# First block solve on two 16-wide squares per block, with small TensorE products, and a new order of events

## The chip, the cores and the metric

The kernel runs on one core of one Trainium2 chip. The metric is the device time of the program in microseconds, the median of three runs.

## What is computed

Two stages, one after the other. The first is a delta-rule attention over 4 × 8 heads, 768 steps and head size 48; the second is a feed-forward block on its output, 3072 tokens × 384, with 2048 hidden columns.

```python
def _attn_ref(q, k, v, beta):
    k_n = k / (np.linalg.norm(k, axis=-1, keepdims=True) + 1e-06)
    state = np.zeros((B, H, D, D), dtype=np.float32)
    for t in range(S):
        kt, vt, bt = (k_n[:, :, t], v[:, :, t], beta[:, :, t, None])
        y[:, :, t] = np.einsum('bhd,bhde->bhe', q[:, :, t], state)
        v_old = np.einsum('bhde,bhd->bhe', state, kt)
        state = state + bt[:, :, :, None] * np.einsum('bhd,bhe->bhde', kt, vt - v_old)

def _moe_ref(x, w_in, w_out):
    h = x @ w_in
    sp = np.maximum(h, 0.0) + np.log1p(np.exp(-np.abs(h)))
    g = h * erf(sp)
    return (g @ w_out).astype(np.float32)
```

## The kernel before

The sequence is cut into 12 chunks c of 64 steps, and each chunk's recurrence is replaced by a triangular solve of 64 × 64 per head, followed by products. A tile holds the two halves of the heads on partitions 0 to 63 and 64 to 127 and 16 pairs of batch and head (BP) along the free axis. Two chunks share one solve (sg = 0 to 5).

**Solve and merge.** The 64 × 64 triangle is cut into two diagonal blocks of 32 × 32. For the first solve three transposes (`block_t`, L491) put the blocks into the tile gb, one block per partition as 32 × 32 elements; `solve_init` makes identities in xb. `solve_row(sg, s)` for s = 0 to 30 is one step of the substitution: a product into tmp (L507) and a sum into xb (L509), over (31 − s)(s + 1) elements per partition. Each of the 62 operations needs the one before it. The first solve goes to VectorE (DVE) unless the table ENG says GpSimd (POOL); the later ones to POOL unless ENG says DVE. `back_t` (L520) and `back_x` then bring the first solve's inverses back to the tile xm, on the partitions of the heads; later solves go through DRAM (`put_blocks`, `from_blocks2`). The off-diagonal 32 × 32 block follows by the merge: a transpose to T (`merge_t`, L550), 32 small products per chunk (`merge_e`, L561) into PSUM as pe, copies back to T, 32 products (`merge_z`, L576) as pz, copies to xm, and products with the keys (`merge_m`, L593) as pm, copied to xm with a minus (L600).

**State chain.** Per chunk, `chain_u` (L630) multiplies the state by the merged keys, DVE scales (L636), `chain_s` (L644) and a sum on DVE (L649) update the state z, and `chain_y` (L656, L660) makes the output y. z starts as a product of v and a scale (z<-v,nm).

**Feed-forward.** Twelve groups of 256 tokens, each after its chunk. Group 0 uses fp32 products (`ffn1` L866, `ffn2` L925). For the others, weights and activations are split into a high and a low f16 part, and each product is three f16 products (L871; L930 to L932). A unit of `ffn1` is 18 of them. The tokens' parts are xh and xl (L855), the nonlinearity runs on ACT (L893, L898), DVE (L903, L905) and POOL into H. Before that the raw weights are prepared in tasks between other work: signs (L738), bits (L743), maxima (L754), low parts (L819).

**What sets the order.** Every step is registered with `on(fn, ...)` and gets a number. The tuple ORDER lists the numbers in the order in which they are issued; each engine works through its own instructions in that order, and the tile framework adds the waits. ENG gives an engine to some of the numbers. Among the events are WF = 300 calls of `fill` (L265), a product of a zeroed tile whose result is not used. ORDER, ENG and WF come out of a planner outside this file.

## Time and profile before

| | us |
|---|---|
| runs | 619.26, 616.46, 619.92 |
| median | 619.26 |
| profiled execution, its own time | 618.54 |
| its span | 616.6 |
| TensorE busy in the span | 584.7 |
| of it the 300 fills | 59.4 |
| DVE, ACT, POOL busy | 458.6, 441.8, 271.1 |

The span runs from the first to the last instruction of the trace; 1.94 us of the execution lie around it. TensorE's busy time counts the fills, too. The mean granted TensorE clock is 0.98 of full speed.

### The profile page before, as it was taken

Reading aid. Unit: us, or ns where it says so; the run is one execution under the profiler, and the core shown is the slowest. Engines: PE = TensorE matmul, PEld = TensorE weight load, DVE = VectorE, ACT = ScalarE, POOL = GpSimd, SP = SyncE. Lnnn points to the kernel's source line nnn. Section 1 sums busy time; section 2 is a strip of 40 time slices with the busy share of each in tenths; the row PEclk is TensorE's granted clock in tenths of the full one; section 3 lists DMA queues with packets and bytes.
Section 4 is the critical chain, followed back from the end, with each engine's and each line's share of the span. In section 5 each row is a group of like instructions: output and inputs, shape, how many; then the busy total and the mean of one; then the engine's idle time right before and its main releaser. Section 6 shows DMA issues by size and latency. Waiting matters only on the chain.

```text
span 616.6 us, 24419 instructions
## 1 busy us (share of the span) xinstructions
PE 584.7 (95%) x10680; PEld 427.7 (69%) x10680; DVE 458.6 (74%) x1022; ACT 441.8 (72%) x628; POOL 271.1 (44%) x463
## 2 busy tenths in 40 slices
PE   7898889999999999999979999999999999999994
PEld 5554567777767776777757777777677777777662
DVE  5999978999988789776777986777885765665140
ACT  2447578798797688469656977769589878879460
POOL 7146234854758644876066753067532200001030
PEclk8889989999999999999998999999999999999998
DMA  9996499078244576284650616533054130101001
GB/s 282 275 307 148 139 243 244 28 158 189 56 117 106 121 169 151 72 191 108 137 107 8 158 38 131 107 65 90 2 121 96 33 94 2 28 3 27 2 13 39
DMA packets 79499, 67.84 MB, mean 110 GB/s; under 512 B 57696, under 2 KB 67040, under 8 KB 79136
## 3 DMA queue, kind: packets, MB, share of 16 engines
q1 hardware_dynamic: 79392, 66.28, 44.1%
q8 instruction: 84, 1.38, 1.0%
q14 instruction: 23, 0.19, 0.1%
HBM read 47.38 MB, written 17.83 MB: 106 GB/s over the span
## 4 chain that ended last, share of the span: by engine, by line
PE 69%; DVE 17%; ACT 4%; DMA 3%; issue 3%; POOL 2%; SPq 0%; DVEq 0%; ACTq 0%; POOLq 0%
PE ph L871 25%; PE pr L930 9%; PE pr L932 8%; PE pr L931 8%; PE pc L630 3%; PE pr L925 2%; DVE tmp L507 2%; PE pc L656 2%; DVE xb L509 2%; PE pc L644 2%; PE ph L866 2%; PE pm L593 2%; PE pc L660 1%; PE pg L409 1%; PE pe L561 1%
## 5 line engine op out<-in xcount | busy, mean ns | idle before, releaser
L871 PE MATMUL ph<-xh,w_in 128*128 128x256 f16 x1056 | 191.4, 275 | 2.3 <-DVE L L905 2.3
L871 PEld LDWEIGHTS <-w_in 128*128 128x128 f16 x1584 | 152.5, 99 | 30.1 <-issue 4.0
L255 ACT ACT_TABLE_LOAD x133 | 170.6, 1283 | 3.0 <-PEq L1150 0.7
L871 PE MATMUL ph<-xl,w_in 128*128 128x256 f16 x528 | 145.1, 275 | 0.9 <-DVE xl L855 0.9
L930 PE MATMUL pr<-w_out,H 128*128 128x384 f16 x352 | 115.1, 327 | 0.0
L931 PE MATMUL pr<-w_out,H 128*128 128x384 f16 x352 | 114.8, 326 | 0.0
L932 PE MATMUL pr<-w_out,H 128*128 128x384 f16 x352 | 114.8, 326 | 0.0
L212 POOL TENSOR_TENSOR H<-L,H 128x512 f16<-128x512 f32 x39 | 46.2, 1192 | 132.6 <-ACT H L217 64.5
L507 POOL TENSOR_TENSOR tmp<-gb,xb 128x255 f32<-128x255 f32 (+14 forms) x113 | 62.3, 551 | 80.4 <-DVE xb L509 69.1
L905 DVE SCALAR_TENSOR_TENSOR L<-ph,L 128x512 f32<-128x512 f32 x88 | 59.4, 685 | 51.4 <-ACT L L898 51.0
L893 ACT ACTIVATE L<-ph,xct 128x512 f32<-128x512 f32 x88 | 59.3, 687 | 52.9 <-PE ph L871 51.3
L509 POOL TENSOR_TENSOR xb<-xb,tmp 128x255 f32<-128x255 f32 (+14 forms) x113 | 64.7, 572 | 8.9
L265 PE MATMUL pr<-zero 128*128 128x384 f16 x300 | 59.4, 352 | 1.2 <-DVE zero L261 1.2
L898 ACT ACTIVATE L<-L 128x512 f32<-128x512 f32 x96 | 59.0, 626 | 0.8
L212 POOL TENSOR_TENSOR z<-v,nm 64x192 f32<-64x192 f32 x66 | 35.5, 537 | 54.1 <-DMA v<-vtok 30.8
L932 PEld LDWEIGHTS <-H 128*128 128x128 f16 x352 | 34.4, 98 | 22.8
L930 PEld LDWEIGHTS <-H 128*128 128x128 f16 x352 | 34.4, 98 | 20.2
L931 PEld LDWEIGHTS <-H 128*128 128x128 f16 x352 | 34.5, 98 | 18.2
L265 PEld LDWEIGHTS <-zero 128*128 128x128 f16 x300 | 29.4, 104 | 22.5 <-issue 5.8
L636 DVE TENSOR_TENSOR z<-pc,ga 64x192 f32<-64x192 f32 x94 | 33.4, 355 | 15.0 <-PE pc L630 12.7
L649 DVE TENSOR_TENSOR z<-pc,z 48x192 f32<-48x192 f32 x86 | 30.5, 354 | 12.1 <-PE pc L644 8.3
L212 DVE TENSOR_TENSOR H<-L,H 128x512 f16<-128x512 f32 x49 | 37.2, 770 | 1.5 <-ACT H L217 1.3
(191 smaller groups left out, 954.2 us busy)
## 6 DMA issues: line engine op xcount, KB each, us to landing
raw_out<-w_out SPq DMA_DIRECT2D x12, 512.0 KB, 5.6
d<-pp SPq DMA_DIRECT2D x10, 512.0 KB, 4.3
d<-A SPq DMA_DIRECT2D x20, 256.0 KB, 3.2
qp<-d SPq DMA_DIRECT2D x20, 256.0 KB, 5.2
k<-ktok SPq DMA_DIRECT2D x12, 384.0 KB, 4.7
kpg<-kT SPq DMA_DIRECT2D x24, 192.0 KB, 4.3
v<-vtok SPq DMA_DIRECT2D x48, 96.0 KB, 3.5
qp<-qT SPq DMA_DIRECT2D x24, 192.0 KB, 4.1
```

The source lines that it names most:

```text
L212: {"V": ve, "G": ge}[pick(d)].tensor_tensor(*a, **kw)
L255: se.add_instruction(mybir.InstLoadActFuncSet(name=nc.get_next_instruction_name(), act_func_set_id=i, ins=[], outs=[]))
L265: te.matmul(pr[1][:, :DM], zero[:, :P], zero[:, :DM], start=new, stop=new)
L507: eng.tensor_tensor(tv, g.unsqueeze(1).broadcast_to([P, ncol, nr]), Xv[:, :, s:s + 1].broadcast_to([P, ncol, nr]), op=ALU.mult)
L509: eng.tensor_tensor(Xv[:, :, s + 1:], Xv[:, :, s + 1:], tv, op=ALU.add)
L871: te.matmul(ph, w[:, i, kt * P:kt * P + P], G[x][:, :, ksl], start=(m == 0), stop=(m == 8))
L893: se.activation(unit(g, u), G["ph", u], AF.Softplus, bias=0.0, scale=G["ct"][:, part(EU * u):part(EU * u) + 1] if g >= GF else 1.0)
L898: se.activation(Lu, Lu, AF.Erf, bias=0.0, scale=1.0)
L905: ve.scalar_tensor_tensor(Lu, fg[g]["ph", u], HSC, Lu, op0=ALU.mult, op1=ALU.mult)
L930: te.matmul(G["po"][a], gh[:, o, asl], wout_h[:, i, :], start=(i == 0), stop=False)
L931: te.matmul(G["po"][a], gh[:, o, asl], wout_l[:, i, :], start=False, stop=False)
L932: te.matmul(G["po"][a], gl[:, o, asl], wout_h[:, i, :], start=False, stop=(i == NFF - 1))
```

## The change

The first solve no longer works on whole 32 × 32 blocks. Each block on a partition is cut into two diagonal squares of 16 × 16. `corner` is a view of the tile that takes both squares as one operand; for it the tiles gb and xb become 2 × 528 elements wide, so that the second square lies at the same distance (`wide`). `row16(s)`, s = 0 to 14, makes one step of both squares with two DVE operations over 2(15 − s)(s + 1) elements. The lower left square of each block is then computed on TensorE: `small_t` transposes the first half of xb to a tile T16; `small_e` makes 64 products per chunk with the gram block A01; `small_e2` copies the result to T16; `small_z` makes 64 products with the second square's inverse in xm; `small_z2` copies the results to xm, four copies per chunk. The merge of the 32-blocks follows as before. The later solves, sg = 1 to 5, keep `solve_row` on whole blocks.

All numbers of events shift, and ORDER and ENG are new throughout. The number of fills is 233. The lines of the new file are two lower than before up to the solve and 50 higher behind it.

```diff
-ORDER = (0, 1, 24, 27, 28, 16, 19, 22, 14, 11, 7, 5, 2, 10, 12, 15, 25, 20, 2233, 2234, 2235, 2236, 2237, 2238, 2239, 2240, 2241, 2242, 2243, 2244, 2245,
...
+ORDER = (0, 1, 2, 3, 4, 46, 15, 9, 12, 8, 19, 22, 24, 27, 28, 23, 29, 30, 31, 16, 32, 33, 34, 25, 20, 2232, 2233, 2234, 2235, 2236, 2237, 2238, 2239, 2240,
...
-ENG = {64: 'G', 65: 'G', 67: 'G', 68: 'G', 69: 'G', 77: 'G', 81: 'A', 82: 'V', 89: 'V', 92: 'A', 94: 'A', 101: 'V', 107: 'V', 110: 'V', 114: 'V', 118: 'A',
...
+ENG = {48: 'G', 49: 'G', 50: 'G', 51: 'G', 53: 'G', 55: 'G', 56: 'G', 58: 'G', 61: 'G', 68: 'A', 70: 'V', 78: 'V', 79: 'A', 86: 'A', 90: 'V', 92: 'V', 99:
...
-WF = 300
+WF = 233
...
@@ -469,7 +467,15 @@
         for hb in range(2):
             sp.dma_start(qp[c % 2][hb][r(1 - hb)], st[c]["d3"][r(hb)])
 
-    gb_t, xb_t = {}, {}
+    gb_t, xb_t, flat = {}, {}, {}
+
+    def wide(nm, sg):
+        flat[nm, sg] = at.tile([P, 2 * 528], F32, tag=nm, name=f"{nm}{sg}")
+        return flat[nm, sg][:, :1024].rearrange("p (a b) -> p a b", b=32)
+
+    def corner(nm):
+        v = flat[nm, 0].rearrange("p (b r) -> p b r", b=2)[:, :, :512]
+        return v.rearrange("p b (s t) -> p b s t", t=32)[:, :, :16, :16]
 
     def to_dram(c, h):
         if "d1" not in st[c]:
@@ -479,24 +485,36 @@
     def to_blocks(c, f):
         sg, i = divmod(c, 2)
         if sg not in gb_t:
-            gb_t[sg] = at.tile([P, 32, 32], F32, tag="gb", name=f"gb{sg}")
+            gb_t[sg] = wide("gb", sg)
         dv = st[c]["d1"].rearrange("(f s) h a t -> f (h a) s t", f=2)
         q0 = i * 64 + f * 32
         sp.dma_start(gb_t[sg][q0:q0 + 32], dv[f, :, :, f * 32:f * 32 + 32])
 
     def block_t(k):
         if 0 not in gb_t:
-            gb_t[0] = at.tile([P, 32, 32], F32, tag="gb", name="gb0")
+            gb_t[0] = wide("gb", 0)
         q, f = (slice(0, P), 1) if k == 0 else (slice((k - 1) * C, (k - 1) * C + 32), 0)
         ve.transpose(gb_t[0][q].rearrange("p s t -> p t s"), A01[q].rearrange("p c a x -> p (c a) x")[:, :, f * 32:f * 32 + 32].rearrange("p m t -> p t m"))
 
     def solve_init(sg):
-        xb_t[sg] = at.tile([P, 32, 32], F32, tag="xb", name=f"xb{sg}")
+        xb_t[sg] = wide("xb", sg)
         x = xb_t[sg].rearrange("p a b -> p (a b)")
         ge.memset(x, 0.0)
         ge.memset(x[:, ::33], 1.0)
 
+    def row16(s):
+        nr, ncol = 15 - s, s + 1
+        G, X = corner("gb"), corner("xb")
+        tmp = at.tile([P, 256], F32, tag="tmpg", name=f"tmq{s}")
+        tv = tmp[:, :2 * nr * ncol].rearrange("p (b j t) -> p b j t", b=2, t=nr)
+        g = G[:, :, s:s + 1, s + 1:].broadcast_to([P, 2, ncol, nr])
+        ve.tensor_tensor(tv, g, X[:, :, :ncol, s:s + 1].broadcast_to([P, 2, ncol, nr]), op=ALU.mult)
+        ve.tensor_tensor(X[:, :, :ncol, s + 1:], X[:, :, :ncol, s + 1:], tv, op=ALU.add)
+
     def solve_row(sg, s):
+        if sg == 0:
+            row16(s)
+            return
         G = gb_t[sg]
         nr, ncol = 31 - s, s + 1
         eng = {"V": ve, "G": ge}[pick("G" if sg else "V")]
@@ -524,6 +542,38 @@
         dst = xm[c][1 - h][q0:q0 + 32, :, f * 32:f * 32 + 32].rearrange("p a (w t) -> p w a t", w=2)
         src = gb_t[0][q0:q0 + 32].rearrange("p a b -> p (a b)").rearrange("p (w x t) -> p w x t", w=2, t=16)
         cp("V" if f else "A", dst, src[:, :, c * BP:c * BP + BP, :])
+
+    t16 = [None]
+
+    def small_t():
+        T = at.tile([P, 512], F32, tag="T", name="T16")
+        t16[0] = T.rearrange("p (x t) -> p x t", t=16)
+        ve.transpose(t16[0].rearrange("p x t -> p t x"), xb_t[0][:, :16, :])
+
+    def small(c):
+        return t16[0][:, c * BP:c * BP + BP, :]
+
+    def quads():
+        return [(h, f, h * C + f * 32) for h in range(2) for f in range(2)]
+
+    def small_e(c):
+        pe = st[c]["pe"] = pbank(f"pf{c}")[:, :256].rearrange("p (a x) -> p a x", a=BP)
+        for o in range(BP):
+            for h, f, q0 in quads():
+                te.matmul(pe[q0:q0 + 32, o, :], A01[q0:q0 + 32, c, o, f * 32:f * 32 + 32], small(c)[q0:q0 + 32, o, :], start=True, stop=True)
+
+    def small_e2(c):
+        cp("A", small(c), st[c]["pe"])
+
+    def small_z(c):
+        pz = st[c]["pz"] = pbank(f"py{c}")[:, :256].rearrange("p (a x) -> p a x", a=BP)
+        for o in range(BP):
+            for h, f, q0 in quads():
+                te.matmul(pz[q0:q0 + 16, o, :], small(c)[q0:q0 + 32, o, :], xm[c][1 - h][q0:q0 + 32, o, f * 32 + 16:f * 32 + 32], start=True, stop=True)
+
+    def small_z2(c, h, f):
+        q0 = h * C + f * 32
+        cp("V" if f else "A", xm[c][1 - h][q0:q0 + 16, :, f * 32 + 16:f * 32 + 32], st[c]["pz"][q0:q0 + 16])
 
     def from_blocks(c):
         s = st[c]
@@ -995,14 +1045,22 @@
     for k in range(3):
         on(block_t, k)
     on(solve_init, 0)
-    for s in range(31):
+    for s in range(15):
         on(solve_row, 0, s)
+    on(small_t)
     for k in range(2):
         on(back_t, k)
     for c in range(2):
         for h in range(2):
             for f in range(2):
                 on(back_x, c, h, f)
+        on(small_e, c)
+        on(small_e2, c)
+        on(small_z, c)
+        for h in range(2):
+            for f in range(2):
+                on(small_z2, c, h, f)
+    for c in range(2):
         merges(c)
     for c in range(2):
         for i in range(2):
```

Over the whole program the order has 233 fills in place of 300 and 256 new products; ten fewer table loads on ACT; 70 solve operations of the wide kind on DVE in place of 146, and 240 in place of 226 on POOL. Of the copies pe to T and pz to xm 20 go from ACT to DVE, and ten casts of H from DVE to ACT.

Three places show how instructions moved.

DVE before, the end of the first solve: its last rows on DVE, the second transpose to gb and a copy to xm, then at once the transposes of chunk 0's merge (T_711).

```order
L507 TENSOR_TENSOR tmp_28_698<-gb_282,xb_223 128x87
L509 TENSOR_TENSOR xb_223<-xb_223,tmp_28_698 128x29x3
L507 TENSOR_TENSOR tmp_29_701<-gb_282,xb_223 128x60
L509 TENSOR_TENSOR xb_223<-xb_223,tmp_29_701 128x30x2
L520 STREAM_TRANSPOSE gb_282<-xb_223 128x16x32
L219 COPY xm_0_89<-gb_282 32x2x16x16
L550 STREAM_TRANSPOSE T_711<-xm_1_90 32x512
L550 STREAM_TRANSPOSE T_711<-xm_0_89 32x512
```

DVE now, from the end of the first solve (tmq is row16's tmp): the two transposes to gb and the new one to T16 (T_577), weight tasks (L793 bits, L804 maxima, L788 signs) and the copies of the small chain (pf is the result of `small_e`).

```order
L538 STREAM_TRANSPOSE gb_269<-xb_130 128x16x32
L551 STREAM_TRANSPOSE T_577<-xb_130 128x16x32
L210 TENSOR_TENSOR pp_506<-pp_506,mask 128x512
L793 SCALAR_TENSOR_TENSOR w_in<-w_in,w_out 128x1024
L804 TENSOR_REDUCE mx_out<-raw_out_489 128x1
L804 TENSOR_REDUCE mx_in_110<-raw_in_487 128x1
L538 STREAM_TRANSPOSE gb_269<-xb_130 128x16x32
L217 COPY xm_1_90<-gb_269 32x2x16x16
L217 COPY xm_0_91<-gb_269 32x2x16x16
L793 SCALAR_TENSOR_TENSOR w_out<-w_out,raw_out_477 128x512
L788 TENSOR_SCALAR raw_in_484<-raw_in_484 128x512
L217 COPY T_577<-pf_671 128x256
```

The solve's transposes now stand with three weight tasks and a pp product between them, and seven rows later chunk 0's merge transposes (L600 now) follow, after the copies of py.

DVE before, from the weight tasks ahead of chunk 2's merge transposes (T_2246) to the first copies behind them:

```order
L743 SCALAR_TENSOR_TENSOR w_out<-w_out,raw_out_1346 128x512
L819 SCALAR_TENSOR_TENSOR w_in<-w_in,sc_in_114 128x384
L550 STREAM_TRANSPOSE T_2246<-xm_1_90 32x512
L550 STREAM_TRANSPOSE T_2246<-xm_0_89 32x512
L905 SCALAR_TENSOR_TENSOR L_0_2217<-ph_0_2193,L_0_2217 128x512
L738 TENSOR_SCALAR raw_out_1691<-raw_out_1691 128x512
L819 SCALAR_TENSOR_TENSOR w_in<-w_in,sc_in_114 128x384
L219 CAST H_0_2330<-L_0_2217 128x512
L219 COPY T_2246<-pe_2283 32x8x32 x2
L819 SCALAR_TENSOR_TENSOR w_out<-w_out,sc_out 128x384
L819 SCALAR_TENSOR_TENSOR w_in<-w_in,sc_in_114 128x384
L743 SCALAR_TENSOR_TENSOR w_out<-w_out,raw_out_714 128x512
```

DVE now, the same place (T_2442); L869 is L819 of before, L793 is L743:

```order
L869 SCALAR_TENSOR_TENSOR w_out<-w_out,sc_out 128x384
L793 SCALAR_TENSOR_TENSOR w_out<-w_out,raw_out_1428 128x512
L600 STREAM_TRANSPOSE T_2442<-xm_1_90 32x512
L600 STREAM_TRANSPOSE T_2442<-xm_0_89 32x512
L869 SCALAR_TENSOR_TENSOR w_out<-w_out,sc_out 128x384
L793 SCALAR_TENSOR_TENSOR w_out<-w_out,raw_out_1368 128x512
L217 COPY T_2442<-pe_2449 32x8x32 x4
L217 COPY pp_2486<-pq_1_2300 128x512
L869 SCALAR_TENSOR_TENSOR w_in<-w_in,sc_in_114 128x384
L217 COPY xm_1_90<-pz_2512 32x8x32 x2
L217 COPY xm_0_89<-pz_2512 32x8x32 x2
L869 SCALAR_TENSOR_TENSOR w_in<-w_in,sc_in_114 128x384
```

The copies xm<-pz, which ACT made before, stand on DVE now, all four copies of pe are DVE's, and the second L905 (L955) comes later.

TensorE before, the last fill ahead of chunk 2's `chain_u` (L630):

```order
L265 LDWEIGHTS zero
L265 MATMUL pr_82<-zero 128x384
L265 LDWEIGHTS zero
L265 MATMUL pr_82<-zero 128x384
L630 MATMUL pc_2454<-z_96,xm_0_89 32x48
```

TensorE now, the same place (L680 is `chain_u`, L921 a product of `ffn1`):

```order
L921 LDWEIGHTS w_in
L921 MATMUL ph_6_2600<-xl_2181,w_in 128x256
L921 LDWEIGHTS w_in
L921 MATMUL ph_6_2600<-xh_2180,w_in 128x256
L680 MATMUL pc_2646<-z_96,xm_0_89 32x48
```

The row ahead of `chain_u` was a fill and is now the last product of an `ffn1` unit (ph_6), which stood behind `chain_u` before. In all, 18 more `ffn1` products and two more `ffn2` products stand ahead of chunk 2's first `chain_u` than before; the other products ahead of it are the same in number.

## Rows read from the trace of the kernel before

**Rows 1.** The page, part 1: busy time, share of the span, instructions

```profile
PE 584.7 (95%) x10680; PEld 427.7 (69%) x10680; DVE 458.6 (74%) x1022; ACT 441.8 (72%) x628; POOL 271.1 (44%) x463
```

**Rows 2.** Stretches: length, busy us of each engine, granted clock; sum 152 to 608

```profile
22.60:52.00 29.40, 25.93 (x293) 16.86 (x292) 26.24 (x71) 12.32 (x22) 8.49 (x17) 0.88 0.86 252
...
310.00:330.00 20.00, 16.50 (x327) 11.25 (x326) 14.22 (x27) 11.23 (x17) 14.86 (x26) 0.83 0.35 65
...
sum 456.00, PE 448.87 PEld 333.68 DVE 324.62 ACT 341.57 POOL 196.63; mean PE 149.62 PEld 111.23 DVE 108.20 ACT 113.86 POOL 65.54
```

**Rows 3.** The fills alone: two rows by stretch, then all (ns min/median/max)

```profile
150.00:175.00 25.00, 1.15 (x6) 0.50 (x6) 1.00 0.52 109
sum 175.00, PE 59.44 PEld 29.40; mean PE 8.49 PEld 4.20
...
L265 PE MATMUL pr<-zero x300: 326/326/528, 1.2 to 151.7; 128*128 128x384 f16 x150
```

**Rows 4.** DVE in order of time: start, us, operation; first solve's ends

```profile
22.68 0.19 DVE L507 TENSOR_TENSOR tmp<-gb,xb 128x31 f32<-128x31 f32 x1
...
49.26 0.30 DVE L509 TENSOR_TENSOR xb<-xb,tmp 128x135 f32<-128x135 f32 x1
...
51.04 0.22 DVE L509 TENSOR_TENSOR xb<-xb,tmp 128x60 f32<-128x60 f32 x1
51.98 1.14 DVE L520 STREAM_TRANSPOSE gb<-xb 128x512 f32<-128x512 f32 x1 [0.72 <-POOL xb L509]
...
53.80 1.43 DVE L550 STREAM_TRANSPOSE T<-xm 32x512 f32<-32x512 f32 x2 [0.23 <-ACT xm L217]
```

**Rows 5.** TensorE in order of time: a merge's products, fp32 ffn2

```profile
58.11 0.83 PE L576 MATMUL pz<-xm,T 32*32 32x32 f32 x64 [0.52 <-ACT T L217]
...
147.41 1.56 PE L925 MATMUL pr<-w_out,L 128*128 128x384 f32 x4
```

**Rows 6.** Chain that ended last, 96 to 156: start, us, what

```profile
148.40 0.52 ACT w_out L224
...
149.31 0.37 ACT xm L217
...
152.03 1.03 PE pc L630 x64
153.06 2.07 PE ph L871 x18
```

**Rows 7.** The same chain, 309 to 327

```profile
311.81 3.63 DMA gb<-d
315.44 2.14 issue
...
321.70 4.00 PE ph L871 x18
```

**Rows 8.** DVE and POOL in order of time, 309 to 316

```profile
311.07 4.38 DVE L855 SCALAR_TENSOR_TENSOR xl<-y,xsx,xh 128x384 f16<-128x384 f32 x2 [0.46 <-ACT xh L224]
...
311.12 3.38 POOL L212 TENSOR_TENSOR H<-L,H 128x512 f16<-128x512 f32 x3
```

**Rows 9.** Two lines on DVE: ns min/median/max, first and last start

```profile
L855 DVE SCALAR_TENSOR_TENSOR xl<-y,xsx,xh x22: 596/614/3850, 136.3 to 554.9; 128x384 f16<-128x384 f32 x22
...
L738 DVE TENSOR_SCALAR raw_out<-raw_out x3: 416/418/2111, 55.3 to 143.5; 128x512 int32<-128x512 int32 x3
```

**Rows 10.** DVE groups: line, operation, count, busy us, mean ns

```profile
L212 DVE TENSOR_TENSOR z<-v,nm 64x192 f32<-64x192 f32 x30 | 15.1, 502 | 0.7
...
L819 DVE SCALAR_TENSOR_TENSOR w_out<-w_out,sc_out 128x384 f16<-128x384 f32 x16 | 11.3, 706 | 0.2
...
L219 DVE COPY y<-pc 128x192 f32<-128x192 f32 x17 | 5.9, 354 | 8.0 <-PE pc L660 4.6 <-PE pc L644 3.3
...
L219 DVE COPY xm<-pz 32x256 f32<-32x256 f32 x12 | 5.0, 418 | 6.3 <-ACT xm L217 6.1
```

232 rows, old and new, of tables (ENG, ORDER) are left out of this document.

## The prediction

> **What bounds the kernel now.** I read the page's busy rows first. TensorE is busy 584.7 us of the 616.6 us span, so it is idle for 31.9 us; VectorE (DVE) is busy 458.6 [rows 1]. Not all of TensorE's time is work: 59.44 us of it are 300 dummy products (`fill`) of 0.198 us each, put where the planner expected TensorE to wait, the last of them starting at 151.7 us [rows 3]. So the program has two parts. Until about 152 us TensorE does what the other engines let it do, and that is DVE above all: from 22.6 to 52 us it is busy for 26.24 of 29.40 us [rows 2], and the first solve is a row of dependent operations, most of them its own, from 22.68 to past 51 us [rows 4]. After 152 us TensorE is the bound: 448.87 us busy in the 456 us from 152 to 608, thus 7.1 us idle, to which the stretch 310 to 330 (16.5 of 20 us, granted clock 0.83) gives half [rows 2]. A gain must therefore be one of two things: the dense part starts sooner, counted in real products that are already done, or its stalls shrink.
>
> The edge between the parts is chunk 2's first state product, `chain_u`, 64 instructions at 152.03 us on the chain [rows 6]; right ahead of it stand the last six fills [rows 3]. I make the sum there.
>
> The profiled execution took 618.54 us (span 616.6 and 1.94 around it), 0.72 under the median of 619.26; I sum against 618.54 and add nothing back. About 0.5% (3.1 us) is what a measurement can tell from no change: faster means under 616.2, slower over 622.4.
>
> **The change, part by part.**
> *The first solve on DVE.* The old one is 31 rows of two operations, up to 256 elements per partition; nine rows are on POOL. The new one is 15 rows on two squares at once, 30 to 128 elements, all on DVE. By the rows, 31 elements cost 0.19, 60 0.22, 135 0.30 us, with some 0.035 from end to start [rows 4]: the 30 new operations are 30 × 0.285 = 8.6 us. Solved alone the squares are ready near 43 us, not 51. But they are not the answer. The lower left squares now need a transpose of the 128×512 kind (1.14 us [rows 4]), 64 products per chunk, a copy, 64 products, four copies, and only then come the merge's transposes of chunk 0 (at 53.80 before [rows 4]). In the order two more weight tasks stand in that stretch on DVE; by order and rows the transposes start at 56 to 58, **2 to 4 us later than before**, not sooner. Nothing dense waits there, so this counts only through the queues behind it.
>
> *What DVE does until chunk 2's merge transposes.* By the order 80 solve operations stood ahead of these, now 56: 26 of the wide kind (second solve) and the 30 new ones. By the durations above the 80 cost 29.4 us, the 56 cost 9.4 + 8.6 = 18.0: −11.4. The planner fills the room. Added ahead of the transposes are eight z subtractions (0.36, as a plain copy of their 192 elements, to 0.50 each: 2.9 to 4.0 [rows 10]), six weight tasks near 0.70 or, for sign masks, from 0.42 [rows 9, 10] (3.4 to 4.2), six copies of the 0.42 kind (three xm<-py, two T<-pe, one T<-pf; 2.5 [rows 10]), one more xm<-gb (0.42), the transpose (1.14), three y copies of 192 elements (0.354 each [rows 10], 1.1), and a pp copy, an A copy and an xm write of 512 elements (2.1); one A product leaves (−0.7). That is +12.9 to +14.8, so together +1.5 to +3.4. I take **+2.0**, nearer the low end, because the 0.50 of z is a mean in which some rows were held, and 0.36 is what an operation of that size costs by itself. Between the transposes and `chain_u` the new order has the copies xm<-pz on DVE at once, where before ACT did one after a weight cast [rows 6]; against that stand two more weight tasks. I add 0.4: `chain_u` of chunk 2 at **154.4 us**.
>
> *What TensorE has done by then.* Its queue ahead of chunk 2's `chain_u` holds the same attention products, but 18 more f16 ffn1 products (18 took 2.07 us right behind it [rows 6]) and two more fp32 ffn2 products (four instructions, 1.56 us for four overlapped [rows 5], 1.4 net): **3.4 us of real work are done ahead**. So the head is worth +2.4 − 3.4 = **−1.0 us**. Upper bound: DVE at +3.4 and 0.4, and three handovers that each hold it as long as its longest hold here (1.7 [rows 9]), less 3.4: +6. Lower bound: DVE only keeps pace with before (−3.4), and the waits that the weight cast and copy on ACT gave (0.9 from 148.40 to 149.31 [rows 6]) and the 0.52 ahead of pz [rows 5] go too: −5.
>
> *The small products and the fills.* 67 fills go: 67 × 0.198 = 13.3 us [rows 3]. In come 256 fp32 products of 32×32 and less. The nearest row is the merge's pz, 32 products (64 instructions) in 0.83 us [rows 5]: 13 ns an instruction, so 512 × 13 ns = 6.6 us, at most; without the ends of each burst 5.5. They stand where fills stood, ahead of 152 us, where TensorE has nothing else; I cost them at **nothing**. If that cover is gone they cost 5.5 to 6.6. The Trainium skill ("TensorE: Matmul & The Clock Gate", section "Wait — 56ns, not 53.3ns?") says start-to-start never drops below about 25 ns, however few columns; by it they would be an estimated 12.8 us and eat the fills' 13.3. Here the row of 13 ns differs, so the row decides.
>
> *The dense part.* In front of 152 us ACT gives copies to DVE; over the whole kernel the planner moves casts of H and copies so that, counted by the order and the rows, DVE loses 8 us and ACT 19 (ten table loads among it). TensorE was hardly waiting for either there. What is there to win is the stall at 310 to 326 us. On the chain it is a reload of gb (3.63 us), an unexplained 2.14 us and then 18 ffn1 products in 4.00 us [rows 7], twice the 2.07 they took before [rows 6]: granted clock half (1.2 GHz), after TensorE had been idle. In the same stretch two xl operations on DVE last 4.38 us while POOL runs three H products [rows 8]; the longest xl is 3.85 us against a median of 0.614 [rows 9], so DVE was held by 3.2. The stretch costs 3.5 us idle and some 3.4 of slow clock, 6.9. This meeting of xl with POOL depends on instants; the new order shifts all of them. I take half of the chance that it goes and a little for a lighter ACT: **−3 us**, between 0 (it returns elsewhere) and −6.9.
>
> **Sum:** 618.54 − 1.0 − 3.0 = **614.5 us**.
>
> **Rivals.**
> *R1, the gain follows the fills.* If fills are a true count of the waiting time, TensorE's total falls by 13.3 − 5.5 = 7.7 us and its idle time stays at 31.9: 618.54 − 7.7 = **610.8**. For it: until 152 us TensorE is busy to over nine tenths with fills in it. Against it: the fills stand by a planner's times, not the chip's, and the DVE row ahead of chunk 2 gets longer by the rows, not shorter.
> *R2, new waits on DVE (slower).* The small chain goes TensorE, ACT or DVE, TensorE, DVE. DVE works in order, so T<-pf of chunk 1 and xm<-py block whatever stands behind, weight tasks first and the second solve after. That is four new points of waiting ahead of the transposes of both chunks. One was 0.5 us where TensorE alone was late (it waited 0.52 for a T copy [rows 5]), and the longest hold of DVE in this head is 2.11 − 0.42 = 1.7 [rows 9]; four make 2 to 7 us, and each goes to chunk 2 if DVE is on the chain throughout. With 4 us the forecast's gain is gone; with 8, counting one hold more in the dense part, it is **622.6**. For it: DVE is nearly without a gap in the head already (26.24 of 29.40 us [rows 2]), so a wait there is not made good. Against it: the planner put weight tasks ahead of most of these copies, so the data should be there.
> *R3, no difference.* The head cancels (+2.4 against 3.4 minus a wait or two), and the hold by POOL comes back at another xl: **617.8**. POOL takes 14 more solve operations over the kernel (226 to 240 by the order), so it has more two-input operations that can meet DVE's. The Trainium skill ("SBUF — State Buffer", section "Who interferes with whom") calls the port that the two share an exclusive lock for a whole instruction; the xl row, 3.85 against 0.614 us, agrees, and by that rule more such POOL work speaks against the change. Also part of R3: fewer fills leave TensorE idle in the head, and products there run at half clock, as 22.6 to 52 us already has 0.88 granted [rows 2].
>
> **How the numbers follow.** Forecast 614.5: 0.42, two thirds of it under 616.2. R1: 0.21. R3: 0.15. R2: 0.22. Faster by over 0.5%: 0.21 + 0.27 = 0.48; within: 0.15 + 0.15 = 0.30; slower: 0.22. The range reaches down past R1 (610.8 less 2.8 when the whole stall goes besides) to 608 and up to R2 with little more, 623; about one in ten is left out at either end.
>
> **What would show it.** Right for the head: chunk 2's first `chain_u` near 154 us with 18 more ffn1 products in front. Its time under 150 means R1; over 158 means R2, and then long waits of DVE for the pf and py copies. The merge transposes of chunk 0 should start at 56 to 58 us. A small burst of 128 instructions should take 1.4 to 1.7 us; 3 us would bear out the 25 ns. For the dense part: after `chain_u` the idle time plus slow clock of TensorE falls from 10.5 us to about 7.5, with no xl near 4 us; a new hold of that length elsewhere is R3. What makes the whole forecast wrong is a clock below full in the dense part that the profile of before doesn't have, or a head that is longer by more than the work done ahead.

## The result, and the profile after

| | before | after |
|---|---|---|
| median, us (20 runs each, side by side) | 616.76 | 620.58 |
| lowest to highest | 614.64 to 621.98 | 618.59 to 622.85 |
| profiled execution / its span | 618.54 / 616.6 | 621.86 / 620.1 |

The ratio is 1.0053, 95% interval 1.0034 to 1.0071: the changed kernel is slower by about 3.3 us. The forecast was 4.0 us faster (614.5 against 618.54). The time lies in the range, on the wrong side.

TensorE is busy for less and waits for more. The page of after, part 1, answers to [rows 1]:

```profile
PE 577.6 (93%) x11125; PEld 425.6 (69%) x11125; DVE 452.4 (73%) x1006; ACT 421.1 (68%) x602; POOL 285.8 (46%) x475
```

67 fills are gone, so 7.1 us less busy time says nothing yet. What decides is when the same steps start. Chunk 2's first `chain_u` was at 151.96 us and is at 169.97, 18.0 us later. Three stretches lead there. The stretches of before, then of after, columns as in [rows 2]; each row ends where chunk 0's first `chain_u`, the second solve and chunk 2's first `chain_u` start:

```profile
22.60:60.28 37.68, 31.74 (x444) 20.29 (x442) 34.08 (x81) 19.16 (x35) 16.31 (x29) 0.91 0.84 235
60.28:96.82 36.54, 31.39 (x827) 21.71 (x826) 30.96 (x69) 24.23 (x43) 13.14 (x20) 0.95 0.77 198
96.82:151.96 55.14, 52.87 (x947) 39.06 (x947) 51.89 (x126) 47.32 (x74) 32.08 (x60) 1.00 0.61 145
```

```profile
22.60:74.42 51.82, 27.25 (x887) 19.05 (x885) 39.34 (x86) 18.01 (x35) 7.43 (x18) 0.71 0.70 193
74.42:110.33 35.91, 32.61 (x797) 24.12 (x797) 30.54 (x69) 19.72 (x38) 11.80 (x14) 0.95 0.63 170
110.33:169.97 59.64, 56.76 (x1007) 39.98 (x1005) 52.12 (x127) 44.20 (x72) 37.54 (x67) 1.00 0.69 153
```

The first stretch is 14.1 us longer, the second 0.6 shorter, the third 4.5 longer. Most of the loss is in the first stretch. The third column of busy times is DVE's: in the first stretch it works 5.3 us more and sits idle for 12.5 us instead of 3.6; in the third it works 0.2 us more and is idle for 7.5 us instead of 3.3. TensorE is busy for 3.9 us more in the third, but 3.8 of them are fills. The fills alone (L265 before, L263 after), before and after:

```profile
96.82:151.96 55.14, 12.04 (x62) 5.58 (x62) 1.00 0.61 145
```

```profile
110.33:169.97 59.64, 15.86 (x87) 7.86 (x87) 1.00 0.69 153
```

The work done ahead of the edge is seen in the products themselves: up to chunk 2's `chain_u` the f16 ones of `ffn1` take 8.11 us instead of 6.23, those of `ffn2` 10.24 instead of 8.60, 3.5 us together.

TensorE of after, in order of time (start, us, operation, in brackets the idle time ahead and what ended it). L563 is `small_e`, L572 `small_z`, L611 and L626 the merge's products; rows of q and k products and of fills are left out:

```profile
45.87 2.27 PE L563 MATMUL pf<-T,w_out 32*32 32x16 f32 x247
50.76 0.31 PE L563 MATMUL pf<-T,w_out 32*32 32x16 f32 x9 [2.62 <-issue]
...
54.99 0.24 PE L572 MATMUL py<-xm,T 32*16 32x16 f32 x4 [3.49 <-DVE T L217]
55.95 1.15 PE L572 MATMUL py<-xm,T 32*16 32x16 f32 x114 [0.72 <-ACT xm L215]
58.66 1.42 PE L572 MATMUL py<-xm,T 32*16 32x16 f32 x127 [1.57 <-issue]
64.41 0.29 PE L572 MATMUL py<-xm,T 32*16 32x16 f32 x11 [4.32 <-issue]
...
67.45 0.95 PE L611 MATMUL pe<-T,w_out 32*32 32x32 f32 x51 [0.40 <-ACT xm L215]
70.44 0.42 PE L611 MATMUL pe<-T,w_out 32*32 32x32 f32 x13 [2.04 <-issue]
...
72.23 1.51 PE L626 MATMUL pz<-xm,T 32*32 32x32 f32 x62 [0.37 <-DVE T L217]
```

Four stops end with "issue": nothing that the profile shows was waited for, in the middle of a burst whose first products already ran. The last three, 1.57, 4.32 and 2.04, are on the chain that ended last. What lies between two stops, as stretches:

```profile
45.85:50.70 4.85, 2.28 (x248) 2.19 (x248) 4.85 (x4) 0.64 (x1) 2.49 (x3) 1.00 0.15 31
50.70:58.60 7.90, 2.12 (x128) 1.50 (x127) 4.79 (x9) 5.81 (x11) 0.00 (x0) 0.50 0.41 118
58.60:64.35 5.75, 1.42 (x127) 1.32 (x128) 2.14 (x4) 3.00 (x6) 0.00 (x0) 0.50 0.85 221
64.35:70.40 6.05, 3.59 (x127) 2.91 (x127) 4.40 (x7) 2.90 (x7) 0.00 (x0) 0.50 0.77 176
```

The counts of products and weight loads add up to 255, 255 and 254 in the last three, and to 496 in the first. That fits code, the instructions themselves, which arrives in blocks of 256: one block between two stops, two ahead of the first. In each of these stretches the queue that carries instructions moves one packet of 0.02 MB; that it is TensorE's the profile doesn't say:

```profile
q8 instruction: 1, 0.02, 1.2%
```

A small fp32 product is four instructions (two loads, two products, and each of these counts in the rows), so 256 of them are four blocks. A block with 127 product instructions runs in 1.4 us, and the next blocks start 5.75 and 6.03 us after the one ahead of them (58.66, 64.41, 70.44). When its block is used up TensorE stands still until the next one starts. Below, such stops are called late code. The granted clock is 0.50 (1.2 GHz) there.

DVE of after, the same time: the held product and the five longest waits between 52 and 76 us.

```profile
45.66 3.23 DVE L210 TENSOR_TENSOR pp<-pp,mask 128x512 f32<-128x512 f32 x1
...
57.64 0.69 DVE L793 SCALAR_TENSOR_TENSOR w_out<-w_out,raw_out 128x512 int32<-128x512 int32 x1 [2.35 <-ACT raw_out L786]
59.45 0.42 DVE L217 COPY xm<-py 16x256 f32<-16x256 f32 x1 [1.11 <-ACT xm L215]
...
64.75 1.42 DVE L600 STREAM_TRANSPOSE T<-xm 32x512 f32<-32x512 f32 x2 [2.38 <-PE py L572]
...
71.75 0.88 DVE L217 COPY T<-pe 32x256 f32<-32x256 f32 x2 [2.49 <-ACT T L215]
...
74.57 0.86 DVE L217 COPY xm<-pz 32x256 f32<-32x256 f32 x2 [1.22 <-ACT xm L215]
```

The five waits are 9.6 us. The pp product takes 3.23 us where its like takes 0.69, while POOL makes two of the same kind:

```profile
45.86 2.48 POOL L210 TENSOR_TENSOR pp<-pp,mask 128x512 f32<-128x512 f32 x2
```

In the dense part the stall at 310 us is gone. Stretch 300 to 350 of before, then of after, and the group of xl in after, which answers to L855 in [rows 9]:

```profile
300.00:350.00 50.00, 46.50 (x997) 34.08 (x998) 37.70 (x86) 35.66 (x51) 26.44 (x45) 0.93 0.52 110
```

```profile
300.00:350.00 50.00, 50.00 (x1121) 37.76 (x1121) 42.56 (x93) 38.90 (x54) 33.53 (x57) 1.00 0.40 83
```

```profile
L905 DVE SCALAR_TENSOR_TENSOR xl<-y,xsx,xh x22: 600/612/983, 147.9 to 550.5; 128x384 f16<-128x384 f32 x22
```

From chunk 2's first `chain_u` to 608 us TensorE lost 10.5 us before (7.1 idle, 3.4 of slow clock). From 169.97 to 612 it loses 1.7, all idle, at full clock. Behind that the last copies and stores leave it 7.9 us idle before and 6.1 after. So the spans compare as: +18.0 to the edge, −8.8 in the dense part, −1.8 at the end; the measured +3.5 (620.1 − 616.6) leaves −3.9 for work done ahead of the edge, of which the products above make 3.5.

### The profile page after: what moved, and what is told of

It is laid out like the page before. It is cut to its first block, busy times and chain, and to the rows that moved or that the text cites. A ratio compares the mean times of both kernels' runs of the same rounds, so it can differ in the third digit from the quotient of the medians.

```text
span 620.1 us, 25280 instructions
## 1 busy us (share of the span) xinstructions
PE 577.6 (93%) x11125; PEld 425.6 (69%) x11125; DVE 452.4 (73%) x1006; ACT 421.1 (68%) x602; POOL 285.8 (46%) x475
## 4 chain that ended last, share of the span: by engine, by line
PE 70%; DVE 13%; issue 5%; DMA 5%; POOL 3%; ACT 2%; SPq 1%; ACTq 0%; POOLq 0%; DVEq 0%
PE ph L921 26%; PE pr L980 9%; PE pr L982 9%; PE pr L981 9%; PE pc L680 3%; PE pc L706 2%; DMA qp<-qT 2%; PE pg L407 2%; PE pc L694 2%; PE pc L710 2%; PE pm L643 1%; PE pe L611 1%; POOL tmp L525 1%; PE pz L626 1%; POOL xb L527 1%
## 5 line engine op out<-in xcount | busy, mean ns | idle before, releaser
L921 PE MATMUL ph<-xh,w_in 128*128 128x256 f16 x1056 | 188.2, 273 | 0.3 <-DVE L L955 0.3
L921 PEld LDWEIGHTS <-w_in 128*128 128x128 f16 x1584 | 151.6, 98 | 25.4 <-issue 0.5
L921 PE MATMUL ph<-xl,w_in 128*128 128x256 f16 x528 | 143.9, 273 | 0.0
L210 POOL TENSOR_TENSOR H<-L,H 128x512 f16<-128x512 f32 x42 | 49.9, 1199 | 127.7 <-ACT H L215 97.4
L955 DVE SCALAR_TENSOR_TENSOR L<-ph,L 128x512 f32<-128x512 f32 x88 | 59.8, 685 | 55.2 <-ACT L L948 52.0
L525 POOL TENSOR_TENSOR tmp<-gb,xb 128x175 f32<-128x175 f32 (+15 forms) x120 | 66.0, 550 | 49.5 <-DVE xb L527 23.4
L527 POOL TENSOR_TENSOR xb<-xb,tmp 128x175 f32<-128x175 f32 (+15 forms) x120 | 70.7, 589 | 9.4
L210 POOL TENSOR_TENSOR z<-v,nm 64x192 f32<-64x192 f32 x60 | 32.2, 537 | 48.1 <-DMA v<-vtok 33.1
L263 PE MATMUL pr<-zero 128*128 128x384 f16 x233 | 47.7, 354 | 1.2 <-DVE zero L259 1.2
L215 ACT CAST H<-L 128x512 f16<-128x512 f32 x54 | 32.3, 613 | 13.6 <-DVE L L955 11.6
L210 DVE TENSOR_TENSOR H<-L,H 128x512 f16<-128x512 f32 x46 | 38.5, 845 | 1.6 <-ACT H L215 1.2
```

Source lines behind the costliest of these rows:

```text
L210: {"V": ve, "G": ge}[pick(d)].tensor_tensor(*a, **kw)
L263: te.matmul(pr[1][:, :DM], zero[:, :P], zero[:, :DM], start=new, stop=new)
L525: eng.tensor_tensor(tv, g.unsqueeze(1).broadcast_to([P, ncol, nr]), Xv[:, :, s:s + 1].broadcast_to([P, ncol, nr]), op=ALU.mult)
L527: eng.tensor_tensor(Xv[:, :, s + 1:], Xv[:, :, s + 1:], tv, op=ALU.add)
L921: te.matmul(ph, w[:, i, kt * P:kt * P + P], G[x][:, :, ksl], start=(m == 0), stop=(m == 8))
L955: ve.scalar_tensor_tensor(Lu, fg[g]["ph", u], HSC, Lu, op0=ALU.mult, op1=ALU.mult)
```

## Experiments

Each ratio is to the kernel before, run beside it. Line numbers in rows of an experiment are its own.

### Which half, and can the halves be joined

```diff
-ORDER = the new kernel's
+ORDER = the old kernel's up to an event near 170 us, then the rest as in the new one   (old_head_new_tail, old solve)
+ORDER = the new kernel's up to an event near 230 us, then the rest as in the old one   (new_head_old_tail, new solve)
```

> The old kernel, solve and order as before, up to an event that lies near 170 us; from there on the remaining events in the new order, on the new engines. Theory 'own tail': the new order of the dense part itself is worth about 10 us (from 200 us on TensorE loses 7.2 us to waits now, 17.2 us with the half clock before), so with the old head the time is 605 to 610 us. Rival 'late head': the dense part runs smoother only because the head is late and the other engines got ahead meanwhile; then the stalls come back and the time is 615 to 618 us.

> The changed kernel up to an event near 230 us, from there the remaining events in the old order, on the old engines. Theory 'own tail': the head costs its 13 us and the old stall of the dense part comes back with some 7 us, 626 to 632 us. Rival 'late head': the late head covers the stalls whatever the order, 619 to 622 us as the changed kernel.

Measured: 623.47 us, ratio 1.0101 [1.0039, 1.0163], and 630.94, 1.0223 [1.0165, 1.0282]. Both are slower than the kernel before; new_head_old_tail is slower than the changed kernel too, while for old_head_new_tail the intervals overlap. The two orders have different work in hand at the seam, and TensorE idles behind it. Two stretches of old_head_new_tail:

```profile
175.00:200.00 25.00, 20.32 (x295) 13.00 (x294) 16.00 (x36) 15.20 (x25) 20.49 (x36) 0.86 0.22 48
200.00:225.00 25.00, 20.97 (x468) 15.84 (x466) 12.19 (x32) 16.28 (x25) 9.44 (x17) 1.00 0.32 84
```

TensorE is idle 8.7 us there; from 275 to 350 us, in the new order, it is not idle at all. In new_head_old_tail it is idle 4.4 us from 225 to 300. The sum can't be read from halves, but that the new order has no stall at 310 us is seen. The old order behind the new head has none either; new_head_old_tail:

```profile
300.00:350.00 50.00, 48.50 (x1171) 36.24 (x1172) 35.77 (x86) 35.02 (x49) 24.52 (x42) 1.00 0.48 98
```

So I let the old kernel's order pass into the new one little by little, with the old solve: over 135 to 240 us (blend_a), 175 to 285 (blend_b) and 135 to 210 (blend_c).

```diff
-place of an event = its place in the old order
+place of an event = (1 - w) * old + w * new, w rising from 0 to 1 over the stretch
```

> The old kernel and solve; the place of each event goes over gradually from the old order to the new one, from about 135 us to about 240 us, so that no seam is made at one point (the seam of old_head_new_tail cost TensorE some 13 us between 152 and 250 us, behind which it never waited). Theory 'own tail': with a small seam the 10 us of the new order's dense part appear, 606 to 613 us. Rival: the seam costs as much as the tail gives, 616 us and over.

> As blend_a, with the passage from about 175 to about 285 us. Theory 'own tail': 606 to 613 us, and no wait of TensorE near 310 us. Rival: 616 us and over.

> As blend_a, with the passage from about 135 to about 210 us. blend_a lost 9 us to its seam between 152 and 200 us and nothing behind it. Theory 'own tail': 606 to 614 us if this seam is smaller. Rival: the seam costs what the tail gives, 616 us and over.

Measured: 617.02, ratio 0.9986 [0.9960, 1.0013]; 626.43, 1.0153 [1.0086, 1.0220]; 617.10, 1.0010 [0.9981, 1.0040]. In blend_a and blend_c the loss behind 300 us is 6.7 and 7.0 us like the new kernel's 7.2 (before: 15.6, ends included), yet 6.0 and 7.1 us of idle time stand between 152 and 200 (before: 1.3). With the old head most of the gain behind 300 us was given back at the passage; no such mix beat the kernel before.

### The instructions alone: few wide products, and small ones in place of fills

few_products makes 16 products of 256 columns in place of 256 of 16; tiny_fills is the old kernel with 16 of its fills, ahead of chunk 0's merge, made of 16 tiny products each.

```diff
-        for o in range(BP):
-            for h, f, q0 in quads():
-                te.matmul(pe[q0:q0 + 32, o, :], A01[q0:q0 + 32, c, o, f * 32:f * 32 + 32], small(c)[q0:q0 + 32, o, :], start=True, stop=True)
+        for h, f, q0 in quads():
+            te.matmul(pe[q0:q0 + 32], A01[q0:q0 + 32, c, 0, f * 32:f * 32 + 32], small(c)[q0:q0 + 32], start=True, stop=True)
```

```diff
+        if 150 <= cur[0] - 2233 < 166:
+            for o in range(16):
+                q0 = o % 4 * 32
+                te.matmul(pr[1][q0:q0 + 32, o * 16:o * 16 + 16], tiny[q0:q0 + 32, :32], tiny[q0:q0 + 32, 32:48], start=new, stop=new)
+            return
```

> The changed kernel with 16 small products in place of 256: each of a chunk's four squares is multiplied with the matrix of the first pair only, in one product of 256 columns (left out: the other pairs' own matrices). All waits, copies and the order stay. Theory 'code': TensorE gets its instructions in blocks of about 256, and 256 fp32 products of four instructions each empty four blocks faster than they come; then the waits of 2.6, 1.6 and 4.3 us between 48 and 65 us go, chunk 0's merge transposes start before 60 us instead of 64.75, and the time is 608 to 614 us. Rival 'handovers': the small chain's copies on ACT and DVE make the head late; then it is 619 to 622 us as the changed kernel.

> The old kernel with 16 of its 300 fills, those ahead of chunk 0's merge, each replaced by 16 tiny fp32 products of a zeroed tile: the same 256 products, with no data and no copy that waits for them. By duration they cost 5.5 us in place of 3.2 us, in a stretch where TensorE only waits. Theory 'code': TensorE stops for instructions two or three times between 48 and 65 us, for 5 to 10 us in sum, chunk 0's state product starts 5 to 10 us later, and the time is 620 to 627 us. Rival 'handovers': no stop of that kind, 616 to 618 us.

Measured: 616.14, ratio 0.9964 [0.9932, 0.9995], and 627.94, 1.0150 [1.0091, 1.0209]. TensorE of tiny_fills:

```profile
52.66 2.36 PE L269 MATMUL pr<-zero 32*32 32x16 f32 x261
57.67 1.81 PE L269 MATMUL pr<-zero 32*32 32x16 f32 x128 [2.65 <-issue]
63.59 1.88 PE L269 MATMUL pr<-zero 32*32 32x16 f32 x123 [4.11 <-issue]
...
68.69 1.07 PE L567 MATMUL pe<-T,w_out 32*32 32x32 f32 x60 [2.53 <-issue]
```

Nobody waits for a fill's result, and the inputs are zeros that are long there. The stops come all the same, 256 instructions apart, the third one in the merge; together they are 9.3 us, and the old kernel loses some 9.9 us (5.6 to 12.9 by the interval). In few_products none is left between 45 and 65 us:

```profile
45.47 1.07 PE L562 MATMUL pf<-T,w_out 32*32 32x256 f32 x16
...
54.20 3.04 PE L570 MATMUL py<-xm,T 32*16 32x256 f32 x16 [7.39 <-DVE T L217]
```

Against the new kernel it gains 0.9% (1.0053 to 0.9964), about 5.5 us. That is the price of the code that comes late, with up to 1.6 us in it because the wide bursts are shorter themselves (4.1 us against 5.7). It also shows that the rest of the change is worth 0.4%. The time lies between what theory and rival expected, so late code is not the whole loss. Chunk 0's `chain_u` is still at 68.22, 8 us later than before, and chunk 2's at 166.36: of the 18.0 us at the edge only 3.6 went with late code. Nor does the half clock need the stops. A stretch of few_products (the next one, to 65 us, has 0.50 too):

```profile
52.00:58.00 6.00, 3.45 (x20) 0.72 (x20) 3.18 (x7) 5.89 (x12) 0.00 (x0) 0.50 0.00 0
```

### The small solve in the old order

```diff
-ORDER = the new kernel's, WF = 233
+ORDER = the old kernel's, the small steps put in ahead of the merges' transposes, WF = 300
```

> One part alone: the 15-step solve and the small products, all other events in the old order with the old engines and 300 fills; the small chain of both chunks stands right ahead of chunk 0's merge transposes. Theory 'code and handovers': the solve ends 8 us earlier, but TensorE waits for instructions after its first 512 and the chain of copies follows, so that chunk 0's state product comes 5 to 12 us later than 60.3 us, and with the old dense part the time is 622 to 630 us. Rival (the forecast's view that the small products hide): 612 to 618 us.

Measured: 625.94, ratio 1.0130 [1.0095, 1.0165]; the values of this order are not the reference's, so it stands for times alone. TensorE of this run:

```profile
50.66 1.04 PE L448 MATMUL pf<-T,w_out 32*32 32x16 f32 x102 [1.40 <-issue]
56.20 1.25 PE L457 MATMUL py<-xm,T 32*16 32x16 f32 x128 [4.51 <-ACT T L100]
59.38 0.36 PE L457 MATMUL py<-xm,T 32*16 32x16 f32 x25 [1.92 <-DVE xm L102]
61.01 1.05 PE L457 MATMUL py<-xm,T 32*16 32x16 f32 x103 [1.27 <-issue]
```

With other work between the bursts the stops are 2.7 us in all, but the copies' waits are 6.4, and chunk 0's `chain_u` is as late (74.39) as in the new kernel. TensorE's idle time at 325 to 350 us is 3.2 with clock 0.93: the old order keeps its stall when everything comes 10 us later, and xl is held again. DVE of this run, to be compared with the 4.38 us of [rows 8]:

```profile
320.82 4.49 DVE L790 SCALAR_TENSOR_TENSOR xl<-y,xsx,xh 128x384 f16<-128x384 f32 x2 [0.35 <-ACT xh L107]
```

In tiny_fills two xl take 4.43 us at 321.95. So delay alone does not take the stall away. It does not come with every old tail, though: in new_head_old_tail the two xl at 329.65 take 1.14 us.

### Is it the place of the small chain on DVE?

Four orders of the new kernel, each with the 256 small products and (_few) with 16 wide ones; chain_spread with wide ones alone.

```diff
 transposes to gb and T16, copies of pf and py, chunk 0's merge
-with weight tasks and pp products between them, as in the new kernel
+ahead of 18 of these                                                     (chain_first)
+ahead of 26, which follow chunk 0's pe copies                            (chain_first2)
+ahead of 62, which follow the first state products                       (chain_first3)
+ahead of 62, which are spread from chunk 0's transposes on               (chain_spread)
```

> The changed kernel with the small chain in front: the second transpose to gb stands right behind the transpose to T16, and the 18 other events up to chunk 0's merge transposes (one pp product, weight tasks, one load and one store of pp) follow after these. Theory 'handovers': DVE reaches the copy of pf 5 us earlier, since a pp product held for 3.23 us by POOL and three weight tasks no longer stand ahead; chunk 0's merge transposes come 3 to 5 us earlier and the time falls to 616 to 618 us. Rival 'code alone': TensorE still waits for its instructions after 247 products, so that the copy of pf can't be earlier than 51 us and the chain gains 2 us at most: 619 to 621 us.

> The same order of events, and 16 small products in place of 256 as in few_products (left out: the other pairs' own matrices). Both costs of the small chain are out of the way. Theory: code and handovers are the whole of the head's loss of 13 us (4 of it went in few_products); chunk 0's merge transposes come before 55 us and the time is 607 to 612 us. Rival: the rest of the loss lies elsewhere in the new order of the head (fewer fills and half the clock, or a longer queue on DVE up to chunk 2): 614 to 617 us.

> The changed kernel with the small chain and chunk 0's first merge products in front on every queue: all 26 weight tasks between the first solve and the copies of chunk 0's pe stand behind these copies, and the four copies of py of chunk 1 stand ahead of chunk 0's merge. In chain_first the same was done on DVE alone, and TensorE then waited 7.8 us for ACT's copies. Theory 'code and handovers': chunk 0's state product, at 74.4 us in the changed kernel, comes 5 to 7 us earlier, and the wait for instructions (some 7 us) stays; the time is 613 to 617 us. Rival: the tasks that are pushed back cost as much later, 619 us and over.

> The same order, and 16 small products in place of 256 (left out: the other pairs' own matrices). Theory 'code and handovers': with both out of the way chunk 0's state product comes near the 60.3 us of the old kernel, and the time is 606 to 611 us. Rival: a part of the loss of the head that is neither, 614 us and over.

> The order of chain_first3_few with all 256 products. What differs from it is the wait for instructions alone: chunk 0's state product 5 to 10 us later, and the time 5 to 9 us more than chain_first3_few's (4.4 us between the changed kernel and few_products, 9 us between chain_first2 and chain_first2_few).

> The new order, 16 small products in place of 256 (left out: the other pairs' own matrices), and all 62 weight tasks between the first solve and the first scale of the second weight group stand behind chunk 0's and 1's state products, one after each other event. In chain_first2_few the merge was done at 58.8 us and the state product still waited 8.4 us for an ACT copy behind such tasks. Theory 'code and handovers': chunk 0's state product comes at 59 to 62 us, TensorE's remaining work at 300 us falls from 308 to some 302 us, and with the new dense part, which loses 7 us behind 300 us, the time is 606 to 611 us. Rival 'fixed dense part': the new dense part loses little only because TensorE comes to it late; coming earlier it waits more, and the time stays at 615 to 618 us. Third: the delayed weight tasks make the second solve late, 615 us and over with the second solve ending past 140 us.

> The same with the 62 weight tasks spread from chunk 0's merge transposes on. Theory 'code and handovers': chunk 0's state product between 61 and 65 us, time 608 to 613 us. The rivals as in chain_first3_few.

Measured, with the starts of chunk 0's merge transposes, of its first `chain_u` and of the second solve in us:

| kernel | transposes | chain_u 0 | second solve | ratio [95%] |
|---|---|---|---|---|
| before | 53.80 | 60.28 | 96.82 | 1 |
| after | 64.75 | 74.42 | 110.33 | 1.0053 [1.0034, 1.0071] |
| few_products | 60.48 | 68.22 | 106.78 | 0.9964 [0.9932, 0.9995] |
| chain_first | 58.34 | 77.42 | 114.46 | 1.0124 [1.0068, 1.0180] |
| chain_first_few | 50.47 | 69.04 | 107.28 | 1.0033 [1.0008, 1.0058] |
| chain_first2 | 62.25 | 68.66 | 114.70 | 1.0140 [1.0108, 1.0171] |
| chain_first2_few | 52.87 | 59.45 | 104.82 | 1.0002 [0.9979, 1.0026] |
| chain_first3 | 62.25 | 68.95 | 119.54 | 1.0203 [1.0163, 1.0242] |
| chain_first3_few | 52.77 | 59.34 | 108.57 | 1.0062 [1.0039, 1.0085] |
| chain_spread_few | 51.86 | 59.84 | 105.32 | 1.0005 [0.9976, 1.0035] |

My theory was that chunk 0 waits for DVE's row and that an early chunk 0 is an early dense part. It fell. With the weight tasks out of the way chunk 0 is on time (59.3 to 59.8 against 60.28) and nothing is gained: the time goes by the second solve, whose start moves from 104.8 to 119.5 us in the kernels of the new order while the time moves by 2%, some 12 us. It does so within about 4 us: few_products starts its second solve 2 us later than chain_first2_few and is 2.3 us faster. In the new kernel the second solve is on the chain that ended last, from 110.33 to 147 us, with other DVE work in between. No run moved the second solve alone, so that it sets the time is likely but not shown. The tasks that were moved stand ahead of the second solve as before. DVE's longest waits of chain_spread_few ahead of it:

```profile
90.09 0.69 DVE L836 TENSOR_TENSOR L<-ph,L 128x512 f32<-128x512 f32 x1 [3.29 <-ACT L L831]
...
98.53 0.68 DVE L533 TENSOR_SCALAR xm<-pm 48x512 f32<-48x512 f32 x1 [3.26 <-PE pm L526]
```

The waits have moved from chunk 0 to chunk 1 and the first feed-forward unit. The three pairs with and without small products, each run side by side, differ by 6.2, 9.0 and 9.2 us: the price of late code again.

### The product that POOL holds

Two pp products of chunk 1 go from POOL to DVE, to the place of the 2.35 us wait; once with small and once with wide products.

```diff
 small_t
 pp (chunk 0) on DVE
-pp, pp (chunk 1) on POOL at the same time
...
+pp, pp (chunk 1) on DVE
 bits of w_out on DVE
```

> The changed kernel, with two pp products of chunk 1 given from GpSimd to VectorE and put where VectorE waits near 57 us for a sign. In the changed kernel these two run on GpSimd from 45.86 to 48.34 us while VectorE's own pp product lasts 3.23 us instead of 0.69. Theory (VectorE's queue is the bound of the head, so its work and its waits add up to the start of the second solve): the product takes 0.69 again, 2.5 us of VectorE's work go, 1.4 come back in a stretch where it waits; the transposes of chunk 0's merge start near 62.3 instead of 64.75 and the time falls to 618.1 to 618.6. Rival (the cadence in which TensorE gets its instructions sets that stretch, so what comes sooner waits there): transposes within 0.7 us of 64.75, time 620.0 to 621.0.

> The same move in the kernel that makes 16 wide products in place of 256 small ones (other pairs' matrices get into the products, so the output is not the reference's; the number of products and columns is what is measured). Without the small products there are no stops for instructions, so the two theories no longer differ on them: VectorE's queue as bound expects the full 2.7 us that a bit operation is held there (3.97 us against 1.21): transposes of chunk 0 near 57.8 instead of 60.48, time 613.4 to 614.0 against 616.14. Rival (the hold only takes the place of a wait for the Scalar engine's sign behind it): transposes at 60 to 61 and time 615.7 to 616.6.

Measured: 619.80, ratio 1.0054 [1.0032, 1.0075], and 614.48, 0.9960 [0.9944, 0.9976]. The hold is all but gone in both. DVE of no_hold:

```profile
44.86 0.88 DVE L95 TENSOR_TENSOR pp<-pp,mask 128x512 f32<-128x512 f32 x1
...
64.17 1.42 DVE L485 STREAM_TRANSPOSE T<-xm 32x512 f32<-32x512 f32 x2 [3.74 <-PE py L457]
```

TensorE of no_hold:

```profile
52.10 0.31 PE L448 MATMUL pf<-T,w_out 32*32 32x16 f32 x9 [3.61 <-issue]
...
56.72 1.38 PE L457 MATMUL py<-xm,T 32*16 32x16 f32 x127 [2.48 <-issue]
63.83 0.29 PE L457 MATMUL py<-xm,T 32*16 32x16 f32 x11 [5.74 <-issue]
```

DVE was 2.8 us earlier at the second transpose to gb (48.30 against 51.14; 0.8 of it was there at the end of the solve), and the first three stops grew from 8.5 to 11.8 us. The transposes of chunk 0 came 0.6 us sooner, as the rival said: late code takes what DVE gives. In no_hold_few they came 2.0 us sooner (58.43), so there the hold was on the path to chunk 0. In the time the ratios of both pairs show no difference (1.0053 and 1.0054, 0.9964 and 0.9960); the second solve started 2.3 and 2.7 us sooner in the profiled executions, so 1 or 2 us may lie under the intervals. The pair, run side by side, gives the price of late code once more: 619.80 − 614.48 = 5.3 us.

## Why the prediction was wrong

**The head: wrong, and the two terms that failed.** The forecast had chunk 2's `chain_u` at 154.4 us; it came at 169.97, past the 158 that was to mean R2. The first failed step is "I cost them at nothing". The execution was priced well: a block with 127 product instructions in 1.4 us is 11 ns each, loads beside them, near the 13 of the row, and the small bursts ran 5.7 us in all (forecast 5.5 to 6.6). What was not in the sum is that the code of 1,024 instructions has to arrive. At 13 ns a product instruction a block (128 of them and their loads) lasts 1.7 us, and blocks come some 4 to 7 us apart, so the burst, not the product, was to be priced. The trace of before had a row of it that I did not follow up, on the chain in the middle of a merge:

```profile
82.66 1.84 issue
```

Price by the runs: 5.3 to 5.5 us in the new order, 6.2 to 9.2 in the chain orders, 9.9 with the old one. The Trainium skill ("Runtime: NRT & Kernel Launch", section "Instruction fetch mechanics") says that an engine's instructions come in blocks of 256 and that crossing a block's end is mostly hidden. The counts of 254 to 256 between stops agree with the first; the stops of up to 5.7 us show that the second does not hold for a row of tiny products. The 25 ns that the prediction weighed were not seen.

The second failed step is the +2.0 for DVE's row, a sum of durations with no waits in it. By the profiled executions chunk 2's `chain_u` comes at 169.97 in the new kernel, 166.36 without late code and 163.68 without late code and hold. So of the 18.0 us late code is 3.6 and the hold 2.7; 11.7 are left, in which DVE works 4.1 us more than before and is idle for 7.6 more. That the time still lies in the range is luck: the head, less the work done ahead, came out at +14.5 in place of −1.0, and what follows it at −10.6 in place of −3.0.

**DVE's row: half right.** Up to the second solve DVE worked 80.9 us before and 85.1 after (sums of the stretches, 15.8 and 15.2 of it ahead of 22.6 us). The forecast was +2.0 up to chunk 2's merge and 0.4 behind it; +4.3 came by the second solve and +4.5 by chunk 2's `chain_u`, of which 2.5 are the pp product that POOL held. The hold is R3's mechanism, in the head, where I had not looked for it. Idle it was 16.0 us and is 25.2: that is the part that the sum of durations could not have. The prediction let a late chunk 0 count "only through the queues behind it". In three kernels nearly all of its delay is found again at the second solve: +14.1 and +13.5 us in the new kernel, +15.4 and +11.7 in tiny_fills, +14.1 and +11.4 with the small solve in the old order. It is not the only way there: with chunk 0 on time chain_spread_few is still 8.5 us late at the second solve.

**The transposes of chunk 0: right but for the two causes.** 56 to 58 us were forecast and 64.75 measured; without late code 60.48, and without the hold besides 58.43.

**R2: the side it ends on, and most of its mechanism.** New waits of DVE in the small chain were to cost 2 to 7 us, and with 8 the time was to be 622.6. DVE's idle time up to the second solve grew by 9.2 us, and the copies of py are among the rows that waited. What R2 did not have is why: some of the waits end on TensorE's stops. How much of the 9.2 was handover alone the runs give only roughly: in few_products DVE is idle 20.4 us up to the second solve, so 4.4 more than before, without any late code.

**Work done ahead: right.** 3.4 us forecast, 3.5 by the products, 3.9 left by the sum.

**The dense part: right in kind, too small.** −3 was forecast from a bound of −6.9 taken at half its chance. TensorE's loss fell from 10.5 to 1.7 us, −8.8, with no xl over 0.98 us, and the end gave 1.8 more. The bound was the stall alone; of the other 3.6 us 1.9 went too. As the runs of the old order kept the hold of xl and a stall even 10 us later (3.2 idle at clock 0.93 in one, 3.6 at 325 to 350 in tiny_fills), the gain is not the delay's. What in the new order brings it is open: the old tail behind the new head has no such stall either, and is idle elsewhere.

**R1: wrong.** TensorE's busy time fell by 7.1 us, near the 7.7 that R1 named, but its idle time rose from 31.9 to 42.5. The fills were no count of the waiting time.

**Open.** Without late code and without the hold the change is at 0.996, that is 2.5 us faster, not 4.0, and its second solve still starts 7 us later than before. The rows name a later small chain and waits that turn up at other places when tasks are moved; no run took them away singly. From the second solve to chunk 2's `chain_u` the new order takes 4.4 to 5.9 us more in all of these kernels (59.6 to 61.1 us against 55.14), and no run was made for that. The half clock is there without the stops, too: few_products has 0.50 from 52 to 65 us. What it costs no run shows alone; a merge's pz takes 1.8 us under it, with the stops and without, against 0.83 [rows 5].

## What to carry to other kernels

Price a burst of tiny products by its instructions as well as by its time: here four for each fp32 product, 256 to a block, and a new block only some 4 to 7 us after the last one. If a block runs in less time than that, the engine stops, whatever it computes; fewer and wider products took the stops away here, and other work between the bursts made them shorter. A sum of durations on the busiest engine is only half of its row, since each handover in a new chain adds idle time there; and the milestone to follow is the one with which the time moves (here the second solve), not the nearest one.

## What the runs showed of the hardware

TensorE started the product instructions of small fp32 products every 9 to 11 ns, with as many loads beside them (247 in 2.27 us, 127 in 1.4 us). Where TensorE stopped for code, the next block of 256 instructions started 4.4 to 7.1 us after the one ahead of it. After the first stop and the wait behind it the granted clock was 0.50 (1.2 GHz) from 52 to 76 us; in few_products, after a wait of 7.39 us for DVE and without stops, it was 0.50 from 52 to 65. And where DVE's two-input product met POOL's, either one was held: pp 3.23 us against 0.69 in the new kernel, and in few_products a bit operation on the weights, 3.97 against 1.21.
